# A speech-joint kernel: weight loads behind accumulating DMAs, a new latency in the planner, operand copies one plane at a time

## The chip, the cores and the metric

The kernel runs on one core of one Trainium2 chip. Its time is the device time of one execution in microseconds (us); less is better. Before the change the median of five runs is 273.85 us.

## The reference

Two strided convolutions, a GELU behind each, and the joint network of a transducer, all in bf16 at the boundaries. B = 2 sequences of T = 4000 frames, D = 512 channels, K = 5 taps, U = 8 labels.

```python
    xp = jnp.pad(x, ((0,0),(pad,pad),(0,0)))
    h = jnp.zeros_like(x)
    for i in range(K):
        h = h + jnp.einsum("btc,cd->btd", xp[:, i:i+T, :], w1[i])
    h = _gelu(h)[:, ::2, :]
    ...
    for i in range(K):
        f = f + jnp.einsum("btc,cd->btd", hp[:, i:i+T1, :], w2[i])
    f = _gelu(f)[:, ::2, :]
    fe = jnp.einsum("btd,de->bte", f, w_f)
    ge = jnp.einsum("bud,de->bue", g, w_g)
    j = jnp.tanh(fe[:, :, None, :] + ge[:, None, :, :])
    return jnp.einsum("btud,dv->btuv", j, w_o)
```

Only every second frame of each convolution is kept, so conv1 gives 2000 frames per sequence and conv2 gives 1000. The output has 2 x 1000 x 8 x 512 values.

## The kernel before

Channels lie on the 128 partitions in NK = 4 blocks, frames along the free dimension. The frames come in by transposing DMAs, sorted by phase (frame number modulo 4 or 6), so that a stride is a choice of planes.

The convolutions are computed with fewer products than the plain five taps need. One sequence's conv1 runs in three tiles that make two outputs at a time from sums and differences of planes (class Tile_). The other sequence's conv1 runs as two objects of class Triple (`first[0]`, `first[1]`), and conv2 of both sequences as two more (`trip[0]`, `trip[1]`). A Triple makes three outputs at a time from nine products: five on planes of its input and four on combinations. Its method `prepare` makes the combinations, and `stages` issues, for each of the four blocks of output channels m, the nine products in PSUM banks e and f. Between the products ScalarE copies a partial sum to `sd` in SBUF, VectorE adds and subtracts, and later products of the same m accumulate on what VectorE wrote back. So TensorE cannot go on with an m until ScalarE and VectorE have done their step. `slot` interleaves three m's to fill those pauses.

For conv2, `prepare` keeps three float32 planes, `r32b`, and each is made in two steps (by_dma): ScalarE writes -2 times one plane of h, and an accumulating DMA on the POOL queue (`acc`, line 597) adds another plane. VectorE then combines the three planes into `row` (trip[0]) or `wide` (trip[1]), which TensorE reads. The transformed conv2 weights are made in the same manner by `w2sums(h)`, for half the output channels at a time: ScalarE writes tap 2 into the float32 buffer `half[h]`, two accumulating DMAs one after the other add taps 0 and 4, ScalarE writes the result to `w2_t` (with the minus sign) or to `w2_sb[2]` (with the plus sign; in the profile w_sb<-half). That is eight accumulates into `half` of 512 KB each and six into `r32b` of 672 KB each. The buffer `r32b` is shared by trip[0] and trip[1], and lies on bytes that `first[0]` has read before.

The joint part needs g, w_g, w_f and w_o. `load_last`, called after `trip[0].prepare()`, issues them on SP's queue. The three weights' buffers (`wg_sb`, `wf_sb`, `wo_sb`) lie where `first[1].prepare` keeps its float32 planes `r32`, so the loads wait for VectorE's last reading of those. `ge` needs w_g and g, `fe` needs w_f, and the output matmuls need w_o; `fe(0)` comes in the last slots of trip[1], and the output stage takes the rest of the time.

The order of work is partly written out and partly planned. Up to `pl.pin = ()` the order on each engine is that of the code. Behind it only TensorE and SP take the ready operation that stands first in the code; ScalarE, VectorE and POOL take the ready operation with the smallest `late`. The class Plan simulates all engines (`simulate`), with a price for each operation, and writes the resulting order into each engine's queue. On the chip each engine then works strictly in that order and waits on semaphores. `late` is found from the end backwards: an operation must be done before the latest allowed start of its successors (line 156: its `span` is its cost, and 4.0 us more if it is a DMA). An accumulating DMA is priced in `simulate` as 1.35 us of issue, 1.0 us, and its bytes at 230e3 bytes per us behind earlier ones of its queue, or at 100e3 while SP's transfers are counted as still in flight:

```python
                soft = max(soft, end + 1.0)
                busy = wire > soft + 1.0
                soft += o.nbytes / (100e3 if busy else 230e3)
                wire += o.nbytes / 220e3 if busy else 0.0
```

The simulation is repeated ROUNDS = 16 times with adjusted `late`, and the order that ends first in the simulation is emitted.

Of the kernel before, what the change touches and what calls it, by code (L numbers as in the profile page):

```python
# [7 lines left out]
ACT = mybir.ActivationFunctionType  # L8
# [3 lines left out]
P = 128  # L12
# [54 lines left out]
class Plan:  # L67
# [76 lines left out]
    def schedule(self, pred):  # L144


        ops, HOP = self.ops, self.HOP
        n = len(ops)
        succ = [[] for _ in ops]
        for i, p in enumerate(pred):  # L150
            for j in p:
                succ[j].append(i)
        late, nextpe = [0.0] * n, 0.0
        for i in range(n - 1, -1, -1):
            o = ops[i]
            span = o.cost + (4.0 if o.dma else 0.0)
            t = min([late[s] - (HOP if pred[s][i] else o.cost - span) for s in succ[i]], default=0.0)
            if o.eng == "pe":
                t = min(t, nextpe)
            late[i] = t - span  # L160
            if o.eng == "pe":
                nextpe = late[i]
        best = None
        for _ in range(self.ROUNDS):
            order, start, end = self.simulate(pred, succ, late)
            if best is None or end < best[2]:
                best = (order, start, end)
            self.urge(pred, order, start, late)
        self.start, self.end = best[1:]
        return best[0]  # L170
# [19 lines left out]
    def simulate(self, pred, succ, late):  # L190


        ops, HOP = self.ops, self.HOP
        n = len(ops)
        left = [len(p) for p in pred]
        ready = [0.0] * n
        free = {e: 0.0 for e in ("pe", "act", "dve", "pool", "sp")}
        cand = {e: [] for e in free}
        for i in range(n):
            if not left[i]:  # L200
                cand[ops[i].eng].append(i)
        order = {e: [] for e in free}
        wire, soft, start = 0.0, 0.0, [0.0] * n
        for _ in range(n):
            best = None
            for e, c in cand.items():
                if c:
                    t = max(free[e], min([ready[i] for i in c]))
                    if best is None or t < best[0]:
                        best = (t, e)  # L210
            t, e = best
            now = [i for i in cand[e] if ready[i] <= t + 0.02]
            i = min(now) if e in ("pe", "sp") else min(now, key=lambda i: (late[i], i))
            cand[e].remove(i)
            order[e].append(i)
            o = ops[i]
            start[i] = t
            free[e] = t + o.cost
            end = free[e]
            if o.dma and e == "pool":  # L220
                soft = max(soft, end + 1.0)
                busy = wire > soft + 1.0
                soft += o.nbytes / (100e3 if busy else 230e3)
                wire += o.nbytes / 220e3 if busy else 0.0
                end = max(soft, end + 2.0)
            elif o.dma:
                wire = max(wire, t + 1.3) + o.nbytes / o.rate
                end = max(wire, t + 2.0)
            for s in succ[i]:
                ready[s] = max(ready[s], end + HOP if pred[s][i] else free[e])  # L230
                left[s] -= 1
                if not left[s]:
                    cand[ops[s].eng].append(s)
        return order, start, max(free.values())
# [75 lines left out]
def bass_standalone__seq2seq_rnn_t_joint__speech_kernel(  # L310
# [35 lines left out]
    DMA0, DMA1 = False, False  # L346
    START = (0, 334, 667, 1000)

    with ExitStack() as es:
# [16 lines left out]
        wf_sb = at("wf_sb", [NK, D], BF16)  # L366
        wg_sb = at("wg_sb", [NK, D], BF16)
        wo_sb = at("wo_sb", [NK, D], BF16)
        r32 = Buf(nc, "r32", [3, NK, 336], FP32, wf_sb.end - wf_sb.bytes)
# [38 lines left out]
        ps = Psum(es.enter_context(nc.psum_tensor("acc", [P, 8 * NT], FP32)))  # L408
        block = es.enter_context(nc.Block(no_gpsimd_drain=True))
        pl = Plan(nc)  # L410
        sub, add = ALU.subtract, ALU.add

        def vec_cost(o, ins, fast=True):
# [10 lines left out]
        def act(o, i, func, scale=1.0, bias=None):  # L424
            rd = (i,) if bias is None else (i, bias)
            pl.op("act", lambda e: e.activation(o.ap, i.ap, func, scale=scale,  # L426
                                                bias=0.0 if bias is None else bias.ap), rd, (o,),
                  o.ap.free_size() * 0.83e-3 + 0.13)
# [22 lines left out]
        def load_w(eng, dst, src):  # L451
            return pl.dma(eng, lambda e: e.dma_start(dst.ap, src), (), (dst,))
# [30 lines left out]
            load_x(1, ph, 0, 512)  # L483
        xall = x.rearrange("b t c -> (b t) c")

        def load_z(i, after=None):
            t0, col = ((0, 16), (331, 0))[i]
            for ph in (4, 0, 2, 5, 1, 3):
                dst = zx[i][ph, :, col:col + 336]
                src = xall[6 * t0 + ph:6 * (t0 + 335) + ph + 1:6, :]  # L490
                o = pl.dma("sp", lambda e, dst=dst, src=src: e.dma_start_transpose(out=dst.ap, in_=src), (), (dst,),  # L491
                           nbytes=336 * D * 2, rate=180e3)
                if after is not None:
                    o.after.append(after.idx)
            if i:
                memset(zx[1][:, :, 336:340])
                memset(zx[1][4:6, :, 335:336])
            else:
                memset(zx[0][4:6, :, 15:16])
# [94 lines left out]
                  vec_cost(o, (a, b), False))  # L594

        def acc(dst, src):
            pl.last_acc = pl.dma("pool", lambda e: e.dma_start(dst.ap, src.ap, accum_op=add), (src, dst), (dst,),  # L597
                   nbytes=P * 4 * dst.ap.free_size())

        def quad(taps, sl, u, v, dst):  # L600
            stt("dve", u, taps[4, :, sl], 4.0, taps[0, :, sl])
# [112 lines left out]
        class Triple:  # L714
# [12 lines left out]
            def z(self, i, d=0, n=None):  # L727
                return self.z_[i, :, self.off + d:self.off + d + (n or self.n)]
# [8 lines left out]
            def prepare(self, by_dma=True):  # L737
                z, n, E, r32 = self.z, self.n, 336, self.r32
                q = lambda j, d=0: r32[j, :, d:d + n]
                at = self.at  # L740
                if by_dma:
                    act(r32[1:3], z(slice(0, 4, 2), 0, E), ACT.Copy, scale=-2.0)
                    act(r32[0], z(4, -1, E), ACT.Copy, scale=-2.0)
                    for i in (1, 2, 0):
                        acc(r32[i], z(2 * i, 0, E))
                else:
                    stt("dve", r32[1], z(0, 0, E), -2.0, z(2, 0, E))
                    stt("dve", r32[2], z(2, 0, E), -2.0, z(4, 0, E))
                    stt("dve", r32[0], z(4, -1, E), -2.0, z(0, 0, E))
                tt("dve", at("t2"), z(4), z(0), sub)  # L750
                tt("dve", at("s1"), z(1), z(3), add)
                act(z(2), z(5, -1), ACT.Copy)
                tt("dve", at("si"), z(5), z(1), sub)
                tt("dve", at("sm"), z(3), z(1), sub)
                o, a, b = at("t1"), q(1), q(2)
                pl.op("dve", lambda e: e.scalar_tensor_tensor(  # L756
                    out=o.ap, in0=a.ap, scalar=-1.0, in1=b.ap, op0=ALU.mult, op1=sub), (a, b), (o,),
                      vec_cost(o, (a, b), False))
                tt("dve", at("t0"), q(2), q(0), sub)
                if self.third:  # L760
                    tt("dve", q(2), q(1), q(2), sub)
                    act(at("tm"), q(2), ACT.Copy, scale=1.0 / 3.0)
                else:
                    tt("dve", at("tm"), q(1), q(2), sub)
                tt("dve", at("ti"), q(0, 1), q(1), sub)
                tt("dve", at("s0"), z(2), z(3), sub)
# [184 lines left out]
        pl.pin = ()  # L951


        def load_rest(after):
            load_z(1, after)
            for i in (0, 1, 3, 4, 2):
                load_w("sp", w2_sb[i], w2[i].rearrange("(k c) d -> c k d", c=P))

        def load_g():
            gd = gT[:]  # L960
            pl.dma("sp", lambda e: e.dma_start_transpose(out=gd.ap, in_=g.rearrange("b u d -> (b u) d")), (), (gd,), nbytes=16384)

        def load_last():
            load_g()
            load_w("sp", wg_sb[:], w_g.rearrange("(k c) d -> c k d", c=P))
            load_w("sp", wf_sb[:], w_f.rearrange("(k c) d -> c k d", c=P))
            load_w("sp", wo_sb[:], w_o.rearrange("(k c) d -> c k d", c=P))

        def bank():
# [37 lines left out]
        for m in range(NK):  # L1007
            slot(tiles[2], m)
            if m == 0:
                first[0].prepare(DMA0)  # L1010
                w1extra()
                load_rest(pl.last_acc if DMA0 else None)
            v = w1_t[1, :, m * P:(m + 1) * P]
            act(v, v, ACT.Copy, scale=0.5)
        for m in range(NK):
# [94 lines left out]
```

## Time and profile before

| | |
|---|---|
| median of 5 runs | 273.85 us (272.83 to 274.55) |
| profiled execution | 274.23 us |
| its span, first to last instruction | 272.1 us |
| mean granted TensorE clock | 0.994 |
| PE busy | 262.3 us (96%), 1582 matmuls |
| PEld (weight loads, beside PE) | 152.5 us (56%) |
| DVE / ACT / POOL busy | 198.5 (73%) / 181.9 (67%) / 20.0 us (7%) |
| DMA queue q1 (SP) | 31.49 MB, 43.0% of 16 engines |
| DMA queue q0 (POOL, accumulating) | 8.32 MB, 16.4% of 16 engines |
| half accumulates, issue to landing | 5.1 / 5.6 / 11.1 us (least, median, most) |
| r32b accumulates, issue to landing | 5.8 / 8.8 / 13.1 us |

The profile is one execution. PE is TensorE's matmuls, PEld its weight loads, DVE is VectorE, ACT is ScalarE, POOL is GpSimd, SP the engine that issues most DMAs; a trailing q names an engine's queue of issues and waits. The page cuts the span into 40 slices of 6.8 us and gives for each the busy share in tenths. The timeline names each instruction with its start and length, and in brackets the idle time of its engine just before it and what ended it. An operation's line is that of the helper that recorded it (L434 all matmuls, L426 all ScalarE operations, L597 all accumulating DMAs), so operations are told apart by their tiles: w_sb stands for w1_sb and w2_sb, w_t for w1_t and w2_t, since numbers are left out of names.

### The profile page before, as it was taken

How to read it: one execution, taken by the hardware profiler on the slowest of the kernel's cores; microseconds unless marked ns; L12 is line 12 of the kernel's file. 1: busy time of each engine (PE TensorE's matmuls, PEld its weight loads, DVE VectorE, ACT ScalarE, POOL GpSimd, SP SyncE). 2: the span in 40 equal slices, each digit the busy share in tenths (PEclk: the TensorE clock that was granted, in tenths of full speed). 3: DMA queues.
4: the chain of work that ended last, by engine and by line, in shares of the span. 5: the costliest groups of instructions: out<-in, count | busy, mean ns of one | idle time of the engine just before them, and what ended most of it. 6: DMA issues, size and time to landing. Idle time of an engine off the chain costs nothing.

```text
span 272.1 us, 4227 instructions
## 1 busy us (share of the span) xinstructions
PE 262.3 (96%) x1582; PEld 152.5 (56%) x1582; DVE 198.5 (73%) x288; ACT 181.9 (67%) x267; POOL 20.0 (7%) x32
## 2 busy tenths in 40 slices
PE   8999999999999939999999999999999999999995
PEld 4997944556656616666766656444444444444442
DVE  0999999999999829939642365667756656667764
ACT  2577955559789747774479967379669769669110
POOL 1000000002543500140000000000000000000000
PEclk9999999999999979999999999999999999999999
DMA  7999999980999990095000130444444444543544
GB/s 250 316 185 198 174 191 171 247 274 19 202 206 221 281 225 3 2 199 108 0 1 2 39 110 8 145 149 154 154 153 154 144 158 148 163 149 133 172 149 143
DMA packets 61985, 40.13 MB, mean 147 GB/s; under 512 B 31742, under 2 KB 61710, under 8 KB 61966
## 3 DMA queue, kind: packets, MB, share of 16 engines
q1 hardware_dynamic: 54430, 31.49, 43.0%
q0 software_dynamic: 7392, 8.32, 16.4%
q8 instruction: 12, 0.20, 0.3%
q10 hardware_dynamic: 144, 0.07, 0.1%
q14 instruction: 7, 0.06, 0.1%
HBM read 7.86 MB, written 16.38 MB: 89 GB/s over the span
## 4 chain that ended last, share of the span: by engine, by line
PE 63%; DMA 18%; issue 8%; DVE 4%; ACT 2%; SPq 2%; POOL 1%; ACTq 0%; POOLq 0%; DVEq 0%
PE acc L434 63%; DMA half<-w_sb 9%; DMA r32b<-hT 2%; DMA zx<-in_x_dram 2%; DMA xs<-in_x_dram 2%; DMA w_sb<-in_w_dram 2%; SPq L465 2%; DMA xr<-in_x_dram 1%; DVE w_t L421 1%; ACT r32b L426 1%; SPq L491 1%; DVE xt L421 1%; DVE hT L421 1%; DVE wide L756 1%; ACT hT L426 0%
## 5 line engine op out<-in xcount | busy, mean ns | idle before, releaser
L434 PE MATMUL acc<-wo_sb,jT 128*128 128x512 bf16 (+1 forms) x504 | 108.4, 377 | 0.0
L1070 DVE CAST ost<-acc 128x512 bf16<-128x512 f32 (+1 forms) x105 | 72.3, 689 | 39.5 <-PE acc L434 39.5
L426 ACT ACTIVATE jT<-feT,geT 128x1000 bf16<-128x1000 f32 (+10 forms) x84 | 72.7, 932 | 16.9 <-PE acc L434 16.9
L434 PEld LDWEIGHTS acc<-wo_sb,jT 128*128 128x128 bf16 x504 | 49.3, 98 | 58.4
L426 ACT ACTIVATE ost<-acc 128x512 bf16<-128x512 f32 (+1 forms) x21 | 12.2, 579 | 22.5 <-PE acc L434 22.3
L434 PE MATMUL acc<-xt,w_sb 128*128 128x252 bf16 (+1 forms) x144 | 23.3, 305 | 0.3 <-DVE xt L421 0.3
L434 PE MATMUL acc<-row,w_sb 128*128 128x334 bf16 (+1 forms) x112 | 19.9, 308 | 0.0
L426 ACT ACTIVATE sd<-acc 128x334 f32<-128x334 f32 (+1 forms) x32 | 14.0, 449 | 8.6 <-PE acc L434 8.1
L426 ACT ACTIVATE hT<-acc 128x334 bf16<-128x334 f32 (+2 forms) x21 | 11.7, 564 | 10.2 <-PE acc L434 10.0
L434 PEld LDWEIGHTS acc<-xt,w_sb 128*128 128x128 bf16 x144 | 13.9, 98 | 6.8 <-DVE xt L421 0.6
L421 DVE TENSOR_TENSOR sd<-sd 128x334 f32<-128x334 f32 (+1 forms) x16 | 8.1, 521 | 10.3 <-ACT sd L426 10.3
L434 PE MATMUL acc<-row,w_t 128*128 128x334 bf16 (+1 forms) x80 | 14.5, 305 | 0.0
L434 PE MATMUL acc<-xs,w_t 128*128 128x252 bf16 (+1 forms) x76 | 13.9, 314 | 0.2 <-DVE w_t L421 0.2
L434 PE MATMUL acc<-fT,wf_sb 128*128 128x333 bf16 (+1 forms) x96 | 14.0, 305 | 0.0
L434 PEld LDWEIGHTS acc<-row,w_sb 128*128 128x128 bf16 x112 | 10.8, 99 | 5.6 <-DVE sd L421 0.2
L592 DVE SCALAR_TENSOR_TENSOR acc<-acc,sd 128x334 f32<-128x334 f32 (+1 forms) x16 | 8.5, 529 | 5.1 <-PE acc L434 5.1
L434 PE MATMUL acc<-zx,w_sb 128*128 128x334 bf16 (+1 forms) x64 | 12.1, 316 | 0.0
L426 ACT ACTIVATE xt<-xs 128x1008 bf16<-128x1008 bf16 (+1 forms) x8 | 10.7, 1350 | 1.8 <-DMA xs<-in_x_dram 1.7
L434 PEld LDWEIGHTS acc<-fT,wf_sb 128*128 128x128 bf16 x96 | 9.3, 97 | 4.5
L990 DVE COPY feT<-acc 128x333 f32<-128x333 f32 (+1 forms) x12 | 7.4, 613 | 5.9 <-PE acc L434 5.9
L434 PE MATMUL acc<-hT,w_sb 128*128 128x334 bf16 x64 | 11.5, 305 | 0.0
L597 POOL DMA_DIRECT2D half<-w_sb x8 | 10.4, 1297 | 14.0 <-DMA half<-w_sb 7.9
(84 smaller groups left out, 346.3 us busy)
## 6 DMA issues: line engine op xcount, KB each, us to landing
out_dram<-ost SPq DMA_DIRECT2D x109, 128.0 KB, 1.9
w_sb<-in_w_dram SPq DMA_DIRECT2D x10, 512.0 KB, 5.4
half<-w_sb POOLq DMA_DIRECT2D x8, 512.0 KB, 5.6
r32b<-hT POOLq DMA_DIRECT2D x6, 672.0 KB, 8.8
xr<-in_x_dram SPq DMA_DIRECT2D x2, 512.0 KB, 4.1
wg_sb<-in_w_g_dram SPq DMA_DIRECT2D x1, 512.0 KB, 6.0
wf_sb<-in_w_f_dram SPq DMA_DIRECT2D x1, 512.0 KB, 7.7
wo_sb<-in_w_o_dram SPq DMA_DIRECT2D x1, 512.0 KB, 11.9
```

Source lines behind the costliest of these rows:

```text
L421: pl.op(eng, lambda e: e.tensor_tensor(out=o.ap, in0=a.ap, in1=b.ap, op=op), (a, b), (o,), vec_cost(o, (a, b)))
L426: pl.op("act", lambda e: e.activation(o.ap, i.ap, func, scale=scale, bias=0.0 if bias is None else bias.ap), rd, (o,), o.ap.free_size() * ...
L434: ins = e.matmul(o.ap, lhsT=l.ap, rhs=r.ap, start=start and n == 0, stop=stop and n == len(pairs) - 1, skip_group_check=not check)
L465: pl.dma("sp", lambda e: e.dma_start_transpose(out=dst.ap, in_=src), (), (dst,), nbytes=(hi - lo) * D * 2, rate=180e3)
L491: o = pl.dma("sp", lambda e, dst=dst, src=src: e.dma_start_transpose(out=dst.ap, in_=src), (), (dst,), nbytes=336 * D * 2, rate=180e3)
L592: pl.op(eng, lambda e: e.scalar_tensor_tensor(out=o.ap, in0=a.ap, scalar=f, in1=b.ap, op0=ALU.mult, op1=add), (a, b), (o,), vec_cost(o, (a ...
L597: pl.last_acc = pl.dma("pool", lambda e: e.dma_start(dst.ap, src.ap, accum_op=add), (src, dst), (dst,), nbytes=P * 4 * dst.ap.free_size())
L756: pl.op("dve", lambda e: e.scalar_tensor_tensor(out=o.ap, in0=a.ap, scalar=-1.0, in1=b.ap, op0=ALU.mult, op1=sub), (a, b), (o,), vec_cost( ...
L990: pl.op("dve", lambda e, o=o, v=v: e.tensor_copy(out=o.ap, in_=v.ap), (v,), (o,), vec_cost(o, (v,)))
L1070: pl.op("dve", lambda e, o=o, v=v: e.tensor_copy(out=o.ap, in_=v.ap), (v,), (o,), vec_cost(o, (v,)))
```

## The change

`load_last` issues g's transpose first, and this DMA now waits for the last three accumulating DMAs recorded, the three of `trip[0].prepare()`. The loads of w_f, w_g and w_o follow on the same queue, with w_f ahead of w_g. In `prepare`, ScalarE's copy of two planes of `r32b` in one instruction becomes two instructions. In the planner the span of a DMA on POOL has 8.0 us in place of 4.0, and the rate of an accumulate while SP's transfers are in flight is 60e3 in place of 100e3. An argument of `load_z` and `load_rest` that was None is dropped; `acc` now collects its DMAs in a list.

```diff
-            span = o.cost + (4.0 if o.dma else 0.0)
+            span = o.cost + ((8.0 if o.eng == "pool" else 4.0) if o.dma else 0.0)
...
-                soft += o.nbytes / (100e3 if busy else 230e3)
+                soft += o.nbytes / (60e3 if busy else 230e3)
...
         def acc(dst, src):
-            pl.last_acc = pl.dma("pool", lambda e: e.dma_start(dst.ap, src.ap, accum_op=add), (src, dst), (dst,),
-                   nbytes=P * 4 * dst.ap.free_size())
+            pl.accs.append(pl.dma("pool", lambda e: e.dma_start(dst.ap, src.ap, accum_op=add), (src, dst), (dst,),
+                   nbytes=P * 4 * dst.ap.free_size()))
...
                 if by_dma:
-                    act(r32[1:3], z(slice(0, 4, 2), 0, E), ACT.Copy, scale=-2.0)
+                    act(r32[1], z(0, 0, E), ACT.Copy, scale=-2.0)
+                    act(r32[2], z(2, 0, E), ACT.Copy, scale=-2.0)
                     act(r32[0], z(4, -1, E), ACT.Copy, scale=-2.0)
                     for i in (1, 2, 0):
                         acc(r32[i], z(2 * i, 0, E))
...
         def load_last():
-            load_g()
+            load_g().after.extend(o.idx for o in pl.accs[-3:])
+            load_w("sp", wf_sb[:], w_f.rearrange("(k c) d -> c k d", c=P))
             load_w("sp", wg_sb[:], w_g.rearrange("(k c) d -> c k d", c=P))
-            load_w("sp", wf_sb[:], w_f.rearrange("(k c) d -> c k d", c=P))
             load_w("sp", wo_sb[:], w_o.rearrange("(k c) d -> c k d", c=P))
```

More of the change, by code (lines that the diff above doesn't have):

```diff
@@ L410, in bass_standalone__seq2seq_rnn_t_joint__speech_kernel @@
         pl = Plan(nc)
+        pl.accs = []
         sub, add = ALU.subtract, ALU.add
@@ L484, in bass_standalone__seq2seq_rnn_t_joint__speech_kernel, with load_z @@
         xall = x.rearrange("b t c -> (b t) c")
-        def load_z(i, after=None):
+        def load_z(i):
             t0, col = ((0, 16), (331, 0))[i]
@@ L490, in load_z @@
                 src = xall[6 * t0 + ph:6 * (t0 + 335) + ph + 1:6, :]
-                o = pl.dma("sp", lambda e, dst=dst, src=src: e.dma_start_transpose(out=dst.ap, in_=src), (), (dst,),
+                pl.dma("sp", lambda e, dst=dst, src=src: e.dma_start_transpose(out=dst.ap, in_=src), (), (dst,),
                            nbytes=336 * D * 2, rate=180e3)
-                if after is not None:
-                    o.after.append(after.idx)
             if i:
@@ L951, in bass_standalone__seq2seq_rnn_t_joint__speech_kernel, with load_rest @@
         pl.pin = ()
-        def load_rest(after):
-            load_z(1, after)
+        def load_rest():
+            load_z(1)
             for i in (0, 1, 3, 4, 2):
@@ L960, in load_g @@
             gd = gT[:]
-            pl.dma("sp", lambda e: e.dma_start_transpose(out=gd.ap, in_=g.rearrange("b u d -> (b u) d")), (), (gd,), nbytes=16384)
+            return pl.dma("sp", lambda e: e.dma_start_transpose(out=gd.ap, in_=g.rearrange("b u d -> (b u) d")), (), (gd,), nbytes=16384)
         def load_last():
-            load_g()
+            load_g().after.extend(o.idx for o in pl.accs[-3:])
+            load_w("sp", wf_sb[:], w_f.rearrange("(k c) d -> c k d", c=P))
             load_w("sp", wg_sb[:], w_g.rearrange("(k c) d -> c k d", c=P))
-            load_w("sp", wf_sb[:], w_f.rearrange("(k c) d -> c k d", c=P))
             load_w("sp", wo_sb[:], w_o.rearrange("(k c) d -> c k d", c=P))
@@ L1011, in bass_standalone__seq2seq_rnn_t_joint__speech_kernel @@
                 w1extra()
-                load_rest(pl.last_acc if DMA0 else None)
+                load_rest()
             v = w1_t[1, :, m * P:(m + 1) * P]
```

## The prediction

> **What bounds the kernel now.** I read the page's 40 slices first, then the waits, the timeline around the one hole in TensorE's row, the chain that ended last, and the queue that issues the loads. Four rows of the slices (6.8 us each):
>
> ```profile
> PE   8999999999999939999999999999999999999995
> ACT  2577955559789747774479967379669769669110
> PEclk9999999999999979999999999999999999999999
> DMA  7999999980999990095000130444444444543544
> ```
>
> TensorE is full from end to end, with one hole in the slice from 95.2 to 102.0 us. Its clock drops in the same slice, and DMA is at 9 in that slice and the four before it. So the time is TensorE's own work plus its holes; outside this hole only gaps of 0.65 us or less are left behind the opening. TensorE's timeline of that place (start us, us, engine, what, and in brackets the idle time before it and its releaser):
>
> ```profile
> 94.27 0.73 PE L434 MATMUL acc<-zx,w_sb 128*128 128x335 bf16 x4
> 94.84 0.73 PE L434 MATMUL acc<-row,w_sb 128*128 128x335 bf16 x4
> 99.75 1.30 PE L434 MATMUL acc<-zx,w_q 128*128 128x335 bf16 x4 [4.18 <-ACT sd L426]
> 100.85 1.33 PE L434 MATMUL acc<-zx,w_sb 128*128 128x335 bf16 x4
> 101.97 0.95 PE L434 MATMUL acc<-row,w_sb 128*128 128x335 bf16 x4
> 102.76 0.73 PE L434 MATMUL acc<-zx,w_sb 128*128 128x335 bf16 x4
> ```
>
> The same stretch in the timeline of all engines, ScalarE's rows of it:
>
> ```profile
> 93.11 0.51 ACT L426 ACTIVATE hT<-sd 128x334 bf16<-128x334 f32 x1
> ...
> 98.31 1.06 ACT L426 ACTIVATE w_sb<-half 128x1024 bf16<-128x1024 f32 x1 [4.69 <-DMA half<-w_sb]
> 99.27 0.43 ACT L426 ACTIVATE sd<-acc 128x335 f32<-128x335 f32 x1
> ```
>
> TensorE waits 4.18 us for a 0.43 us eviction into sd. That eviction has its data, but ScalarE works in order and the instruction ahead of it, w_sb<-half, waits 4.69 us for an accumulating DMA. The chain of waits shows what those DMAs cost from issue to landing (start us, us, what):
>
> ```profile
> 70.82 5.06 DMA half<-w_sb
> ...
> 78.34 6.09 DMA half<-w_sb
> ...
> 88.86 9.42 DMA half<-w_sb
> ```
>
> 5.06 us early, 9.42 us at the hole. Between lie these three issues on SP's queue:
>
> ```profile
> 83.17 0.37 SPq L452 DMA_DIRECT2D wg_sb<-in_w_g_dram  x1
> 83.58 1.16 SPq L452 DMA_DIRECT2D wf_sb<-in_w_f_dram  x1
> 84.79 1.81 SPq L452 DMA_DIRECT2D wo_sb<-in_w_o_dram  x1
> ```
>
> The page's DMA issues say that they landed 6.0, 7.7 and 11.9 us after issue, so they share the DMA engines with the accumulates from about 85 to 96.7 us. The stretch from 84 to 95 us has a DMA share of 1.14 (full: 17 us before it, without these loads, have 1.12). The first matmul on wg_sb is at 126.3 us, on wf_sb at 137.0, on wo_sb at 151.7: nothing needs these loads so early.
>
> **Part 1: the joint loads wait for the three accumulates into r32b of the first conv2 triple.** What it takes out is 3 x 512 KB of traffic ahead of those accumulates. I rebuild the POOL queue without it, in the order of before. A lone 512 KB accumulate takes 5.08 us; behind another one it lands about 2.5 us after it (198 GB/s in the stretch from 67 to 84 us make 2.65; the rate of r32b's makes 2.3). The r32b ones of the second triple, undisturbed, landed 5.8, 8.0 and 9.6 us after issues at 114.56, 115.31 and 116.79, so 3.0 us apart.
> - half 0's second tap-0 accumulate lands at 84.43 as before; half 1's, issued at 81.21, at 84.43 + 2.5 = 86.9 (before: 7.4 us after issue, 88.6).
> - half 0's last, issued at 84.71: 89.8 (before 95.8). Half 1's last is issued at 87.2 and lands at 92.3 (before 98.28).
> - r32b's remaining two: 95.3 and 98.3. Before, the first took 11.3 us from 89.61, so 100.9; the second some 3 us more.
>
> ScalarE's w_sb<-half is reached at 93.6, after the 92.3 landing: the 4.69 us wait is gone, and TensorE's 4.18 with it. The clock goes along: the 12 matmuls from 99.75 to 102.76 took 3.01 us, while the rows before the hole start four matmuls every 0.57 us, so 1.71 for 12. That is 1.30 us more. Sum 5.48.
>
> The granted clock was 0.87 from 96 to 100 us and 0.70 from 100 to 104, and 1.00 on either side. The Trainium skill (TensorE: Matmul & The Clock Gate, "Part 1: The HAM clock gate") says that the clock halves after an idle window of about 3.4 us and comes back after about as long a time of work. By the page alone that ramp would cost 1.7 us, an estimate, and the sum would be 5.9.
>
> What is late next? VectorE's row<-r32b instructions, from 103.46 on, need r32b: they move up by 5.5 to 98.0, the one that needs both late pieces from 104.92 to 99.4, against landings at 95.3 and 98.3. About 1.1 us of cover, so conv2 can start 5.5 us earlier too. TensorE still has 32 matmuls of conv1 behind the hole, 4.6 us, to bridge.
>
> Where the wait is added: SP. It now holds g's transpose (2.39 us of issue, which was out at 53.9 us) and the three loads behind it; behind those are only output DMAs, from 153.65 us on. From 98.3: g's issue to 100.7, then the loads. The five w2 loads, issued from 50.15 to 52.43, landed 5.2 us (the first) to 8.7 us (the last) after issue, so some 1.5 us apart: wf lands about 106, wg 107.5, wo 109. First uses, moved up by 5.5: wg at 121, wf at 131, wo at 146. Cost 0, hidden under conv2's matmuls; without that cover it would be at most the 10.7 us that the loads take. Swapping wf and wg costs nothing with it.
>
> The Trainium skill's own page (Trainium Kernel Development and Optimization, "Best Practices") tells to overlap DMA with compute, which speaks for issuing loads early and so against this change. Here the early load buys nothing that a row needs and takes the place of transfers that TensorE waits for; by the rule the sum would be 0 or a loss.
>
> **Part 2: ScalarE's operand copy in two planes.** 128x2688 in 2.47 us becomes two of 128x1344 at 1.32 to 1.34: 0.17 us more ScalarE work in each of two places, beside TensorE. The first accumulate may be issued 1.1 us earlier. In the second triple this shortens the chain r32b copy (111.83), DMA (114.56), hT, wide, after which TensorE has 0.18 us idle at 125.29: minus 0.18.
>
> **Part 3: the planner's numbers.** The longer latency (8 against 4 us) only ranks work ahead of accumulates earlier on ScalarE, VectorE and POOL; the 60e3 rate holds only while SP's traffic is counted as in flight, which is now mostly after the accumulates. No row prices a new order. The nearest: at 80.02 TensorE idled 0.65 us because ScalarE waited 0.53 us for a half that nothing disturbed. The planner's price of a lone one (1.35 + 1.0 + 2.28 + 0.16 = 4.79) is 0.3 short of 5.08, and four follow each other. Bounds: minus 0.65 (that gap goes as well) to plus 3. I take plus 0.65, one more such gap, since it is the row for undisturbed accumulates.
>
> Sum: 4.18 + 1.30 + 0.18 - 0.65 = 5.0 us off. The profiled execution took 274.23 (span 272.1 and 2.1 around it) and becomes 269.2; it lies 0.4 over the median of 273.85, so the median becomes 268.8.
>
> **The rivals.**
> - Part of the wait comes back (0.19). With the loads gone the planner takes every accumulate for undisturbed and puts its readers on ScalarE and VectorE as early as its short price allows. For: the 80.02 row, and TensorE's lack of slack. Against: landings now agree with its price within 0.3 us each. Four in a row are 1.2 us; with r32b's three and some clock, 1.2 to 3 us on top: 270 to 271.9.
> - The loads collide with the second triple's accumulates (0.14, slower). Place: these accumulates, issued at 107 to 108 once all moves up. If the first triple's land only at 103, where they land now, the loads travel until 113, and the first r32b takes 11.3 us (as at 89.61) where it took 5.8. TensorE then stands 5.5 us at the chain that ends at 125.29, and its clock drops again, 1.3: 6.8 - 5.0 = 1.8 us worse than before, 275.6. It decides once wo lands later than about 110; I have 109, so the margin is thin, but one late microsecond costs about one.
> - It does not do what it says (0.05): accumulates are slow at 85 to 98 for another reason, such as POOL's issue. For: POOL sat idle 2.2 and 2.9 us there. Against: those idles are waits for the accumulates themselves, and 5.8 us is back at 114.56. Time: 273.85, no change.
>
> **How the numbers follow.** The forecast has 0.62. Its own ends: all gaps gone, 4.18 + 1.30 + 0.18 + 0.65 = 6.3, so 267.5; the runs shown scatter by some 0.7 about the median, so 266.8 is the low end. Upward the range takes the first rival whole and ends at 272.3; the other two, 0.19, are left out but for their edges. About 0.5% (1.4 us) is what a measurement of this kernel can tell from no change. Faster: 0.62 and 0.17 of the first rival, 0.79; within it 0.07; slower 0.14.
>
> **What would show it.** Right: no ScalarE wait for half over 1 us, no TensorE gap over 1 us between 30 and 130 us, a granted clock of 1.0 from 90 to 110, half's landings at 5 to 6.5 us, the joint loads issued near 98 to 101 and landed before 110, the steady stretch of output matmuls starting some 5 us earlier. Wrong: a new hole ahead of a row<-r32b or wide<-r32b instruction, r32b landings of 9 us and more while SP's loads are in flight, or a hole behind a ScalarE copy that was ranked ahead of an sd eviction.

## The result, and the profile after

The changed kernel takes 270.94 us (median of 41 runs, 270.04 to 272.13), the kernel before 273.76 (78 runs, 270.70 to 276.45). The ratio is 0.992, interval 0.9905 to 0.9933: 0.8% faster, clear of the noise. That is 2.2 us by the ratio and 2.8 by the medians, since the ratios leave out executions more than 1.5% above the fastest of their kernel and the medians do not. The forecast was 5.0; the time itself lies in the range given. The profiled execution took 270.63 us; its span is 268.8 us, 3.3 less than before.

The slices of the page, to be laid beside those of before:

```profile
PE   7999999999999988999999999999999999999995
ACT  2767975459778697854489965579669769669110
PEclk9999999999999999999999999999999999999999
DMA  7999999890996998940000130443544444443544
```

The 3 in TensorE's row has become two 8s, and the clock never drops. The DMA row has a 6 where it was full (slice from 81 to 87 us): the queue of accumulates runs dry there once; from 84 to 86 us the DMA share is 0.00. TensorE's timeline behind the opening, the rows with idle time before them:

```profile
69.39 0.74 PE L435 MATMUL acc<-zx,w_q 128*128 128x334 bf16 x4 [0.49 <-ACT sd L427]
...
83.15 0.74 PE L435 MATMUL acc<-zx,w_q 128*128 128x335 bf16 x4 [0.16 <-ACT sd L427]
...
96.03 0.74 PE L435 MATMUL acc<-zx,w_q 128*128 128x335 bf16 x4 [1.32 <-ACT sd L427]
...
102.17 0.74 PE L435 MATMUL acc<-hT,w_t 128*128 128x334 bf16 x4 [0.70 <-DVE hT L422]
...
114.14 0.74 PE L435 MATMUL acc<-hT,w_t 128*128 128x334 bf16 x4 [0.40 <-ACT sd L427]
```

They sum to 3.07 us. Before it was 0.65 + 4.18 + 0.18 and 1.30 for the clock, 6.31. The difference, 3.24, agrees with the span's 3.3. So one hole was removed, and new ones came. ScalarE and VectorE just ahead of the largest (first ScalarE's timeline, then VectorE's):

```profile
93.47 1.32 ACT L427 ACTIVATE hT<-hT 128x1336 bf16<-128x1336 bf16 x1 [1.61 <-DMA r32b<-hT]
...
95.54 0.44 ACT L427 ACTIVATE sd<-acc 128x335 f32<-128x335 f32 x1
```

```profile
93.54 1.55 DVE L422 TENSOR_TENSOR row<-r32b 128x1336 bf16<-128x1336 f32 x1 [2.00 <-DMA r32b<-hT]
```

It is the same pattern as before with another DMA: a reader at the head of an in-order queue waits for an accumulate, and the eviction that TensorE needs (95.54) stands behind it. This DMA is the second of the three accumulates into r32b of the first conv2 triple, and the first of the two that are late; the text below calls it r32b's first late piece. It was issued at 85.19 and landed 8.3 us later. The order of POOL's accumulates in the changed kernel shows why:

```profile
78.56 1.28 POOL L596 DMA_DIRECT2D half<-w_sb  x1 [3.56 <-ACT half L427]
84.43 1.28 POOL L596 DMA_DIRECT2D half<-w_sb  x1 [4.60 <-DVE ws L591]
85.19 1.83 POOL L596 DMA_DIRECT2D r32b<-hT  x1
85.94 2.39 POOL L596 DMA_DIRECT2D half<-w_sb  x1
87.44 2.19 POOL L596 DMA_DIRECT2D r32b<-hT  x1
95.75 1.28 POOL L596 DMA_DIRECT2D half<-w_sb  x1 [6.12 <-DMA half<-w_sb]
```

The first two are both of the same half, so that the second waits for the first's landing (84.15, 5.6 us after issue; the row names VectorE's ws, on which this accumulate does not depend) with everything behind it in POOL's queue. Then four accumulates go out within 3 us and queue behind each other. Before, the halves took turns. The loads are where the change puts them:

```profile
98.36 1.49 SPq L961 DMA_TRANSPOSE gT<-in_g_dram  x1
99.90 0.58 SPq L453 DMA_DIRECT2D wf_sb<-in_w_f_dram  x1
100.52 0.51 SPq L453 DMA_DIRECT2D wg_sb<-in_w_g_dram  x1
101.07 0.51 SPq L453 DMA_DIRECT2D wo_sb<-in_w_o_dram  x1
```

### The profile page after: what moved, and what is told of

It is laid out like the page before. It is cut to its first block, busy times and chain, and to the rows that moved or that the text cites. A ratio compares the mean times of both kernels' runs of the same rounds, so it can differ in the third digit from the quotient of the medians.

```text
span 268.8 us, 4229 instructions
## 1 busy us (share of the span) xinstructions
PE 260.6 (97%) x1582; PEld 150.9 (56%) x1582; DVE 198.5 (74%) x288; ACT 181.9 (68%) x269; POOL 20.0 (7%) x32
## 4 chain that ended last, share of the span: by engine, by line
PE 72%; DMA 12%; DVE 6%; issue 4%; SPq 2%; ACT 2%; POOL 2%; POOLq 0%; DVEq 0%
PE acc L435 72%; DMA r32b<-hT 6%; DMA half<-w_sb 2%; DMA xs<-in_x_dram 2%; DMA w_sb<-in_w_dram 2%; SPq L466 2%; POOL half L596 2%; DMA xr<-in_x_dram 1%; DVE hT L422 1%; DVE row L422 1%; DVE xt L422 1%; DVE row L756 1%; ACT hT L427 0%; DVE w_t L422 0%; DVE sd L422 0%
## 5 line engine op out<-in xcount | busy, mean ns | idle before, releaser
L596 POOL DMA_DIRECT2D half<-w_sb x8 | 11.8, 1494 | 18.1 <-DMA half<-w_sb 8.9
L435 PE MATMUL acc<-hT,w_t 128*128 128x334 bf16 x64 | 11.4, 305 | 1.1 <-DVE hT L422 0.7
```

What stands on the lines that cost most here:

```text
L435: ins = e.matmul(o.ap, lhsT=l.ap, rhs=r.ap, start=start and n == 0, stop=stop and n == len(pairs) - 1, skip_group_check=not check)
L596: pl.accs.append(pl.dma("pool", lambda e: e.dma_start(dst.ap, src.ap, accum_op=add), (src, dst), (dst,), nbytes=P * 4 * dst.ap.free_size()))
```

## The experiments

Each ratio of x1 to x15 is against the kernel before, on the same chip in the same rounds; its median there was 273.3 to 273.5. The runs were spread over three chips, so ratios are the safer comparison between them. Intervals that overlap leave a difference of a microsecond open.

| run | median us | ratio, 95% interval |
|---|---|---|
| changed kernel | 270.94 | 0.992 (0.9905 to 0.9933) |
| x1_order_before_wait | 268.27 | 0.983 (0.979 to 0.988) |
| x2_order_after_no_wait | 273.22 | 1.000 (0.997 to 1.003) |
| x3_wait_only | 270.06 | 0.989 (0.984 to 0.994) |
| x4_planner_only | 274.93 | 1.006 (1.003 to 1.009) |
| x5_after_span4 | 269.61 | 0.987 (0.983 to 0.991) |
| x6_after_nosplit | 270.81 | 0.992 (0.989 to 0.994) |
| x7_after_price | 268.90 | 0.984 (0.980 to 0.989) |
| x8_price_span4 | 267.44 | 0.980 (0.976 to 0.984) |
| x9_readers_later | 270.67 | 0.991 (0.987 to 0.994) |
| x10_price_nosplit | 268.91 | 0.986 (0.983 to 0.990) |
| x11_price_nowait | 270.08 | 0.990 (0.987 to 0.993) |
| x12_before_span8 | 273.06 | 1.001 (0.998 to 1.005) |
| x13_small_half | 268.48 | 0.982 (0.979 to 0.985) |
| x14_price16 | 268.38 | 0.981 (0.977 to 0.984) |
| x15_price14 | 268.58 | 0.982 (0.979 to 0.985) |

**The wait and the order taken apart.** Two of the four runs here keep an order that the planner made for another kernel: the list is emitted unchanged, only waits are added or removed.

```diff
         order = self.schedule(pred)
+        for i, js in self.extra:
+            pred[i].update((j, True) for j in js)
```

This is x1's edit on the kernel before, cut to its core: `extra` names g's transpose and the three accumulates of `trip[0].prepare()`, for which it now waits.

> The order of every engine of the kernel before, kept to the instruction; only g's transpose and the three joint loads behind it wait for the three accumulates of the first conv2 triple. Theory (the loads made the hole; what the change lost again comes from its new order): half's last accumulate lands near 92 us in place of 98, TensorE's hole of 4.2 us and the clock's drop are gone, gaps behind the opening sum to 1.5 us or less, 268.5 to 269.5 us. Rival (the planner's price is short by some microseconds in any order, so that waits of 1 to 3 us stay whatever the loads do): 270.5 to 272 us, with a gap of over 1 us near 95 us.

It took 268.27 us, 0.2 under the theory's range and far from the rival's. All of TensorE's gaps behind 30 us are these two:

```profile
79.16 0.74 PE L437 MATMUL acc<-zx,w_b 128*128 128x335 bf16 x4 [0.68 <-ACT sd L429]
...
118.97 1.31 PE L437 MATMUL acc<-wide,w_sb 128*128 128x334 bf16 x8 [0.18 <-DVE wide L759]
```

Its accumulates, from 80.34 on:

```profile
80.34 1.28 POOL L600 DMA_DIRECT2D half<-w_sb  x1 [1.55 <-ACT half L429]
83.79 1.28 POOL L600 DMA_DIRECT2D half<-w_sb  x1 [2.16 <-DMA half<-w_sb]
86.34 1.28 POOL L600 DMA_DIRECT2D half<-w_sb  x1 [1.28 <-DMA half<-w_sb]
87.09 3.14 POOL L600 DMA_DIRECT2D r32b<-hT  x2
```

The last row holds two DMAs. The five landed 5.7, 6.4, 5.7, 7.8 and 9.9 us after issue, at 86.1, 90.1, 92.0, 94.9 and 97.8. ScalarE reaches w_sb<-half at 92.64 and does not wait.

> The order of every engine of the changed kernel, kept; g's transpose and the joint loads no longer wait for the accumulates, so that the loads go out once VectorE has read r32, near 83 us. Theory (the loads cost the accumulates beside them 4 to 5 us): the first r32b piece lands near 97 in place of 93.4, ScalarE's hT copy and VectorE's row wait 3 to 5 us longer, 273.5 to 276 us. Rival (the new order made the gain, not the wait): 271 to 272 us, like the changed kernel.

The other way round: the changed kernel's own order with the wait deleted from `pred` after planning. 273.22 us, a little under the theory's range and far from the rival's. The loads are issued at 82.4 to 83.4, r32b's first late piece lands at 95.4 (9.8 us after issue) and not at 93.4, VectorE's row waits 3.96 us and ScalarE's w_sb<-half 3.73. So the wait is worth 2.3 us even in the poorer order.

> The wait of the joint loads (and wf ahead of wg) alone, planned anew with the planner's old numbers (4 us, 100e3) and the copy of two planes in one instruction. Theory (the split and the 8 us brought the order that queues half 1's last accumulate behind r32b's, and the waits at 93 us): 268.5 to 269.5 us, faster than the changed kernel by 1.5 to 2.5. Rival (any order planned on the short price leaves such waits): 270.5 to 271.5 us, like the changed kernel.

The changed kernel with `4.0`, `100e3` and `act(r32[1:3], ...)` put back. 270.06 us, between the two ranges: 0.6 above the theory's and 0.4 below the rival's. The waits are those that the rival names. POOL's halves take turns here, as before, and half's last lands at 92.15 as in x1, and yet ScalarE waits 2.09 us for it, VectorE 2.20 us for r32b, and TensorE 1.28 us at 94.87. So the split and the 8 us are not needed for such waits. A new plan is enough: the accumulates land as in x1, other readers stand in front of them, and 1.8 us are lost by the medians (the intervals of x1 and x3 overlap).

> The planner's two numbers alone (8 us and 60e3) on the kernel before; loads early, copy in one instruction. With 60e3 a half accumulate beside the loads is priced at 8.7 us in place of 5.2, so the planner no longer puts ScalarE's w_sb<-half ahead of evictions that TensorE waits for. Theory (the loads' traffic is what costs): a part of the hole stays, since the data still come late, 271 to 273.5 us, the r32b landings at 100 to 104 us as before. Rival (the numbers of the planner made the gain): 270.5 to 271.5 us.

The first two edits of the change, put on the kernel before. (The 8.7 and 5.2 us of the expectation are the price of the bytes alone.) 274.93 us, slower than before and above both expectations. ScalarE still waits 3.88 us for half and TensorE 2.91 us at 97.78; smaller gaps of 0.4 to 0.8 us come at 79.9 to 83.2. The planner's numbers alone bring nothing and cost some 1.5 us.

**Which part of the new order costs.**

> The changed kernel with the planner's old latency of 4 us for accumulating DMAs; all else as changed. Theory P (in every order planned anew, readers of accumulates stand too early in ScalarE's and VectorE's queues, since a lone accumulate is priced 0.5 us short and they follow each other): 269.5 to 271 us, gaps of 1 us in the neighbourhood of 95 us stay. Rival E (the 8 us made the bad order): 268 to 269 us.

`8.0` back to `4.0`: 269.61 us, in theory P's range. The largest gap left is 1.35 us, at 98.52, behind VectorE's wait of 1.81 us for r32b.

> The changed kernel with the copy of two planes in one instruction again, so that r32b's second accumulate can't go ahead of half 1's; all else as changed. Theory P: 269.5 to 271.5 us, with ScalarE waits of 1 to 2 us for half or r32b. Rival S (the split made the bad order): 268 to 269 us, POOL alternating between the halves, no wait of ScalarE or VectorE for r32b over 0.5 us.

`act(r32[1:3], ...)` back in one instruction: 270.81 us, in P's range. ScalarE waits 2.68 and VectorE 2.44 us for r32b, more than P's 1 to 2 us; but the profiled execution is the slowest of the twelve (272.36), so these waits are the high end.

> The changed kernel with one number altered: the fixed part of an accumulate's price is 1.5 us in place of 1.0, so that a lone 512 KB one is priced 5.1 to 5.3 us, as it is measured (5.06 to 5.26). Theory P: readers are queued later, the waits of ScalarE (1.61) and VectorE (2.00) for r32b fall under 0.6 us, TensorE's gaps behind the opening sum to 1.5 us or less, 268.3 to 269.7 us. Rivals S and E: the split and the 8 us are still there, so 270.3 to 271.5 us.

```diff
-                soft = max(soft, end + 1.0)
+                soft = max(soft, end + 1.5)
```

268.90 us, in P's range, with the split and the 8 us still in place. VectorE's wait of 2.00 for r32b is down to 0.35, ScalarE's is 0.75, and TensorE's gaps behind the opening are 0.30, 0.47 and 0.78; ScalarE's wait and the sum of the gaps, 1.55, are a little over the bounds.

> The changed kernel with the fixed part of the price at 1.5 us and the latency back at 4 us. Theory P: gaps behind the opening under 1 us in all, 267.8 to 269 us, as good as the order of before with the wait (268.3) or better. Rival S (the split's order loses 2 us by itself): 270 to 271 us.

267.44 us, the lowest median: 2.0% under the kernel before and 0.4 below the range expected. Against x1 it is not shown to be faster, since the intervals overlap. TensorE's gaps behind 30 us are 0.19 and 0.33.

This run shows where the price acts. POOL issues its accumulates in the same pattern as in the changed kernel (two of one half, r32b, the other half, r32b; the names do not tell which half or plane goes first) and within 0.3 us of the same times: 84.59, 85.34, 86.09, 87.46 and 95.82. r32b's first late piece lands at 93.1, in the changed kernel at 93.4. What differs is who stands in front of it. VectorE's rows:

```profile
93.13 0.85 DVE L422 TENSOR_TENSOR hT<-hT 128x1336 bf16<-128x1336 bf16 x1 [0.37 <-DMA r32b<-hT]
...
97.11 1.54 DVE L422 TENSOR_TENSOR row<-r32b 128x1336 bf16<-128x1336 f32 x1
```

The first row<-r32b, at 93.54 after a wait of 2.00 in the changed kernel, comes at 97.11 without one. ScalarE's first w_sb<-half comes at 96.48 (89.72) and its hT copy at 98.52 (93.47). With the landings nearly the same, the place of the readers made the difference. The longest wait of this run, VectorE's 2.67 us for r32b at 113.71, has no gap of TensorE behind it: a wait for an accumulate costs only where something that TensorE needs stands behind it.

**Readers and landings in the changed kernel's own order.** A plan with another price is another order, so the next two keep the changed kernel's.

> The order of every engine of the changed kernel, but for three readers of the first conv2 triple: ScalarE's hT copy that waits 1.61 us for r32b is queued three instructions later, behind the next sd eviction; VectorE's row<-r32b that waits 2.00 us is queued four later, and the hT difference that needs ScalarE's copy three later. Prices, loads and accumulates are as in the changed kernel. Theory P (the gap is made by the place of the readers, not by the time of the landing): TensorE's 1.32 us ahead of 96.03 falls under 0.4, r32b still lands near 93.4, 269.6 to 270.2 us. Rival (TensorE has no other work by then, so that it waits for r32b wherever the readers stand): 270.6 to 271.4 us with the gap a little later.

```diff
         order = self.schedule(pred)
+        for e, i, n in self.later:
+            q = order[e]
+            k = q.index(i)
+            q.insert(k + n, q.pop(k))
```

`later` holds the three readers with the 3, 3 and 4 places by which they move.

270.67 us: the rival's range. The gap at 96.03 is gone, and r32b's first late piece landed at 93.5 as in the changed kernel, but TensorE's timeline now has these:

```profile
98.41 0.74 PE L439 MATMUL acc<-row,w_sb 128*128 128x335 bf16 x4 [0.75 <-DVE sd L426]
...
102.00 0.74 PE L439 MATMUL acc<-hT,w_t 128*128 128x334 bf16 x4 [1.13 <-DVE hT L426]
```

VectorE still stood idle 1.73 us before 94.19, for an sd that TensorE had not yet fed, since nothing else that it could do was queued there; from there it is busy without a break, and TensorE waits for it twice. The gaps sum to 3.15 us, as much as in the changed kernel (3.07). Moving three readers moves the gap; the plan of x8, which moves the work around them too, does not have it.

> The changed kernel with every engine's order kept; the eight accumulates into half move two of four channel blocks each (the other two are left out), so that they land about 1.1 us sooner each, and r32b's with them. Theory P (the changed order loses its time because accumulates land later than it was planned for): r32b's first piece lands by 92, VectorE's 2.00 us and ScalarE's 1.61 us waits shrink below 0.7, TensorE's gaps behind the opening sum to 1.5 us or less, 268.3 to 269.5 us. Rival (the order itself is too full on VectorE, whatever the landings): gaps of 2.5 us and more stay, 270.2 to 271 us.

```diff
-            acc(v, w[0])
-            acc(v, w[4])
+            acc(v, w[0], 2)
+            acc(v, w[4], 2)
```

The same edit stands a second time for the plus sign. The 2 is the number of channel blocks that the DMA moves, so this kernel leaves out half of the sums; its order and prices are those of the changed kernel.

268.48 us, theory P's range. With the order as it was and earlier landings (r32b's first late piece at 90.64 and not at 93.44), VectorE and ScalarE no longer wait at that place, and TensorE's gaps behind the opening are

```profile
69.22 0.74 PE L435 MATMUL acc<-zx,w_q 128*128 128x334 bf16 x4 [0.49 <-ACT sd L427]
...
99.37 0.74 PE L435 MATMUL acc<-hT,w_t 128*128 128x334 bf16 x4 [0.20 <-DVE hT L422]
...
111.30 0.74 PE L435 MATMUL acc<-hT,w_t 128*128 128x334 bf16 x4 [0.37 <-ACT sd L427]
```

1.06 us in all, in place of 3.07. So in this order it is the landings that cost: 2.8 us sooner is enough to take the waits and two thirds of the gaps away. x8 shows the same from the other side, with late landings and later readers.

**Price without the wait, and how much is chance.**

> The kernel before with the fixed part of the price at 1.5 us alone; the loads go out early and share the DMA engines as before. Theory (the loads' share is the larger cost, and 0.5 us more in the price does not cover landings that come 4 to 6 us late): a hole of 2 us or more stays, 271.5 to 274 us. Rival (an honest price is enough, and the loads need not wait): 268 to 270 us.

The `1.5` alone on the kernel before: 270.08 us, a miss; it comes close to the rival. The loads still go out at 83 to 85 and the accumulates beside them take up to 13.1 us, but the readers stand late enough that TensorE loses 1.41 and 0.74 us in two places instead of the hole. The longer price by itself is worth about as much as the whole change under study (ratios 0.990 and 0.992), and the wait adds 1.2 us to it (x10).

> Wait of the joint loads and the fixed part of the price at 1.5 us, with the copy in one instruction and 4 us. Against x8_price_span4 this is the split alone. Theory (the split is worth little: 0.2 us more ScalarE work, r32b 1 us earlier): 267.2 to 268.5 us, within 0.7 of x8. Rival S (the split costs or brings over 1 us): outside that.

268.91 us against x8's 267.44. The expectation calls this the split alone, but the run also has the rate back at 100e3, where x8 keeps 60e3. So the 1.5 us belong to the split, to the rate or to the order that came of them, and no run parts them; between x6 and the changed kernel (270.81 and 270.94) the split alone brought nothing.

> The kernel before with the latency of 8 us in place of 4 alone. Theory (the 8 us cost 1.3 to 1.5 us in each pair so far: 270.9 against 269.6, 268.9 against 267.4): 274 to 275.5 us. Rival (it is neutral, and the pairs differ by chance of the order): 272.8 to 273.9 us.

273.06 us: the rival. The 8 us cost 1.3 and 1.5 us in two pairs (x5 against the changed kernel, x8 against x7) and nothing in this one. x4, which adds the 60e3, took 274.93.

> x8_price_span4 with 1.6 in place of 1.5 us in the price. Nothing that the chip does is meant to differ but the order. Theory (with a price that is long enough the orders planned are all good): 267.2 to 268.2 us, within 0.6 of x8. Rival (an order's time is chance by more than 1 us either way): outside that.

> x8_price_span4 with 1.4 in place of 1.5 us in the price. Theory: 267.3 to 268.5 us, within 0.9 of x8. Rival (an order's time is chance by more than 1 us either way): outside that.

268.38 and 268.58 us, both faster than before by 1.8 to 1.9% and both 0.9 to 1.1 above x8, a little outside the ranges expected. By the ratios the three lie only 0.1 to 0.3% apart, inside their intervals, and x8 ran on another chip. So a tenth of a microsecond in a price may move the time by up to 1 us through the order alone, and differences of 1 us between planned orders, those of the split and of the 8 us among them, are not put down to a cause here. The price of 1.5 stands above that: it gained 2.0 (x7 against the changed kernel), 2.2 (x8 against x5) and 3.4 us (x11 against the kernel before). The fourth pair, x10 against x3, gives 1.2 us in the same direction, with intervals that overlap. The neighbours at 1.4 and 1.6 lie within about a microsecond of 1.5.

## Why the prediction was right in kind and wrong in size

- **The bound.** Right. The time is TensorE's work and its holes: the spans of the kernel before, the changed kernel and x1 differ by their gaps, the clock's loss and up to 0.9 us in the opening.
- **Part 1, the loads' share.** Right, and shown by x1, in the order for which it was worked out. Forecast landings: 86.9, 89.8, 92.3, 95.3, 98.3; measured 86.1, 90.1, 92.0, 94.9, 97.8, with all of x1 about 0.9 us earlier from the opening on. Counted from there, four of the five came 0.4 to 1.2 us later than forecast (half 0's last took 6.4 us and not 5.08), and the cover was enough. The 4.18 and the clock's 1.30 went. The profiled span fell by 6.4 us: 0.9 in the opening, which is luck, and 5.5 behind it, where 5.48 was forecast. The medians fell by 5.2.
- **The wait's cost on SP.** Right: nothing. g's issue took 1.49 us and not 2.39; the loads landed 4.0, 4.9 and 5.8 us after issue, so wf by 103.9 and wo by 106.9 (I had 106 and 109).
- **Part 2.** The 0.17 us of ScalarE work is there (six copies of 1.31 to 1.34 us in place of two of 2.44 to 2.47 and two of 1.32 to 1.34), but no gap of TensorE can be put down to it. The 0.18 ahead of the second triple did not simply go; 0.40 stands at 114.14 in the changed kernel, behind a ScalarE copy that waited 1.25 us for a first accumulate of 6.6 us, not 5.8.
- **Part 3, the new order.** This is the step that failed, by its size. I took plus 0.65, from the one gap in a plan that already existed. Measured, the changed kernel against x1: 270.94 - 268.27 = 2.7 us, which takes in the order that the split brought. These 2.0 us more are nearly all of the 2.1 by which the forecast of 268.8 missed the time. The bound of plus 3 held. The row at 80.02 was the wrong one to choose: it is a gap of an order that suits the landings, as x1 shows, and a new order need not. Each plan made anew on the old price with the wait (x3, x5, x6 and the changed kernel) had a longest wait of 1.8 to 2.7 us for an accumulate. The argument that landings agree with the price within 0.3 us held for lone accumulates only: in the changed kernel half's at 85.94 took 9.5 us and r32b's two late ones 8.3 and 10.9, queued behind each other. That the short price adds up along half's two-deep chains and in POOL's queue is the likely way; it was not followed step by step. That a longer price takes most of the gaps away is shown (x7, x8).
- **The rivals.** The first, "part of the wait comes back", names what happened, at 0.19: its time was 270 to 271.9. Its argument, readers placed "as early as its short price allows", is what x7, x8 and x13 bear out. The collision of the loads with the second triple did not come: wo landed near 106.9, before the limit of 110. In x5 and x7 the triple's first accumulate was issued at 106.64 and 103.72, while wo still travelled (landed at 107.9 and 105.6), and took 5.7 and 5.8 us as without the loads. That accumulates were slow there for another reason than the loads is excluded by x1's landings.
- **The signs.** Of those named for right, the clock, ScalarE's waits for half (0.90 at most) and the times of the loads came. TensorE's gap of 1.32, half's landing after 9.5 us and the first output DMA at 150.39, only 3.3 us earlier, did not, and these are the signs of Part 3.
- **The kernel before** is not one time, so that the gain by the ratio is smaller than that by the medians. In its 78 executions beside the experiments the mean granted clock tells two groups apart: 19 at 1.000 took 271.02 to 272.62 us (median 271.67), 59 at 0.986 to 0.994 took 272.78 to 275.87 (median 273.78). The profiled one, at 0.994, is of the second group. All executions of the changed kernel are at 0.998 or more. So the clock's term was there to be won in most executions of the kernel before, not in all; how long the hole is in the first group no profile shows.

The ramp of the clock was weighed between the row's 1.30 us and the Trainium skill's rule (TensorE: Matmul & The Clock Gate, "Part 1: The HAM clock gate"), which made it 1.7 as an estimate. In x1 hole and ramp went together, but profiles with shorter holes show the ramp by itself. This is TensorE in the profile of x6 (four matmuls take 0.57 us at full clock):

```profile
99.16 0.74 PE L435 MATMUL acc<-hT,w_t 128*128 128x334 bf16 x4 [2.01 <-DVE hT L422]
99.74 1.25 PE L435 MATMUL acc<-row,w_sb 128*128 128x335 bf16 x4
100.78 1.33 PE L435 MATMUL acc<-zx,w_sb 128*128 128x335 bf16 x4
101.90 1.32 PE L435 MATMUL acc<-row,w_sb 128*128 128x334 bf16 x4
103.02 0.83 PE L435 MATMUL acc<-hT,w_t 128*128 128x334 bf16 x4
```

The sixteen matmuls from 99.74 end with the next row's start at 103.69: 3.95 us in place of 2.28, so 1.67 lost. The granted clock is 0.50 from about 99.8 to 103.2, 3.4 us. x2 and x4 lose 1.68 and 1.69 us in the same way, also in 3.4 us. In the kernel before the clock is at 0.50 from 99.0 to 102.4, again 3.4 us, but TensorE starts only at 99.75: the first 0.75 us fell into the hole, where they cost nothing, and half of the other 2.65 us is the row's 1.30. So row and rule agree, and the row, which has the hole in it, was the right one to use. The idle time that it takes is another matter: in x6 a hole of 2.01 us and in x2 one of 2.55 was followed by the drop, in x12 one of 2.89 was not, so an idle time of 3.4 us is not what decides here; what does is open.

## What to carry to other kernels

When a planner with written prices lays down in-order queues, look at what its prices say of the slowest producers, and compare with the trace: here 0.5 us in one number was worth as much in a new plan as moving the transfers (3.4 us each by the medians, x11 and x3), and the versions with both are 1.4 and 2.0% faster (x10, x8). To price a change that makes such a planner plan anew, don't take the gaps of the order that exists: here the old order with the new wait lost 2.7 us less than the new one. And to learn what the change itself does, emit the old order with the new waits: that run took the forecast apart at once.

## What was not expected

- Chance of the order: up to 1 us (0.4%) by the medians between plans whose prices differ by 0.1 us (267.44, 268.38, 268.58); by the ratios it is not clear of the noise.
- The first accumulate of the second triple took 5.8 us in all eight profiles with the copy of two planes in one instruction, and 5.6 to 6.9 us in the nine with two (6.6 in the changed kernel, issued at 105.48). In x13 it took 6.6 us, issued at 102.67 when wo had landed (102.6), so the loads are not the reason; what is was not tried.
- SP's issue of the same three loads took 0.37, 1.16 and 1.81 us in the kernel before and 0.58, 0.51 and 0.51 in the changed one. The accumulates beside it do not explain that: in x2 and x11 the loads go out beside accumulates too, and took 0.37, 0.56, 0.51 and 0.37, 0.51, 0.57.
